# An attention and gated-MLP kernel: the first batch's weight preparation, the sums of its tiles, LayerNorm's small operations and the last batch's order

## The chip, the cores and the metric

The kernel runs on one core of one Trainium2 chip. Its five engines work in parallel, each through its own instructions in order: TensorE (PE in the profile; its weight loads are PEld), VectorE (DVE), ScalarE (ACT), GpSimd (POOL) and SyncE (SP), whose queue issues all DMAs here. The metric is the device time of one execution in microseconds (us); the median of three runs is given.

## What is computed

Eight batches of block-causal attention (8 heads, 576 positions, 64 per head), then a gated MLP with a spatial mixing matrix. Cut to what matters:

```python
scores = q @ k.T / 8                      # per batch and head, masked by blocks of 64
attn = exp(scores - max) ; attn = attn / (sum(attn) + 1e-9)
x = attn @ v                              # heads side by side: 576 x 512
h = maximum(x @ w_in, 0)                  # 512 -> 1024
u, v = h[:, :512], h[:, 512:]
v_n = (v - mean(v)) / sqrt(var(v) + 1e-6)
v_s = w_spatial @ v_n + b_spatial[:, None]
out = (u * v_s) @ w_out                   # 512 -> 512
```

w_in and w_out arrive as 64-bit floats. The kernel splits every operand of the MLP's matrix products into a high and a low part and adds three products (high x high, high x low, low x high).

## The kernel before

**Pairs and tiles.** Heads go in pairs: 8 batches x 4 pairs, numbered 0 to 31 here. A pair has nine score tiles (TILES, line 45): one for both heads' last 64 queries, and four of 128 queries for each head.

**Batch 0's attention** is a loop over 36 tiles (lines 821 to 845). Each step n issues one tile (`scores`, line 286: matmul, then on VectorE the masked maximum, on ScalarE the exponent with its row sum, on VectorE an addition and a reciprocal, on GpSimd the division), a few steps of "background" work, and the transposes of the tile five steps back (three from step 30 on). `av_lo` and `av_hi` make x of the pair. The two smallest tiles of a head share one sum; each other tile has its own. The order of these instructions on an engine is left to a scheduler that works by priority and estimated times.

**Background.** `spread` gives a generator a first and a last step. v's columns of w_in are prepared in steps 5 to 28, u's in 34 to 37, w_spatial in 40 to 47, w_out in 46 to 52; the last two fall behind the loop. Each block of 128 rows is loaded into one of two staging buffers (`stage`, tags gh and gl, which later hold the gates), decoded by four VectorE instructions (lines 152 to 165), cast on ScalarE (129) and subtracted on GpSimd (131).

**Batches 1 to 7's attention.** For a pair, `scores_8` (two matmuls, L518) is issued during the groups of the pair before, `scores_run` (L540) issues the other eight tiles in a row; `top` (L487, L494) takes maximum and exponent, `norm` (L502, L505, L508) the sums and the division. `turn_blocks` transposes on VectorE (L579 to L588), `regroup` moves the result by four DMAs on SP (L595, pb to ptt), and `av_pair` (L607) of that pair follows the scores of the next one. Scores and av take PSUM banks from a ring of six (`bank`, line 469), so av's first matmul waits until VectorE has read the bank's former scores.

**The MLP of a batch** runs in groups of matmuls between the scores of the next batch: five v groups (`v_group`; the fifth, v4, for the last 64 positions, L651), eight u groups (`u_group`, L711), eight spatial groups (`sp_group`, L735 to L740) and eight output groups (`out_group`, L761), the last two in halves z. A v group goes on in later calls: statistics (L662, L663 on VectorE), then logarithm and exponent on ScalarE (L665, L666) and four operations of one column on VectorE (L667 to L679), then the normalisation (L684), a cast (L690) and the low part on GpSimd (L691). The groups share two PSUM banks. A spatial group's result is multiplied with u (L742), cast (L745) and subtracted (L746) into gh and gl, which the output groups read.

`issue` (line 851) calls one group and takes the groups behind it one step further; `in_order` chains the instructions of each engine by hand in the order in which they were written, without the background's. `moe` returns the groups by pair. For batch 0 those are [v0, v1, v2, u0, v4], [v3, u1 to u5], [u6, u7, four spatial], [four output, four spatial], and four output groups for the next batch's first pair. Pair 4's scores stand ahead of the first v group.

Of the kernel before, what the change touches and what calls it, by code (L numbers as in the profile page):

```python
# [51 lines left out]
def kernel(  # L52
# [66 lines left out]
    staged = []

    def stage(name):

        tag = ("gh", "gl")[len(staged) % 2]
        staged.append(name)
        t = ff_p.tile([P, ND, HT], F32R, tag=tag, name=f"r{name}")
        return t.bitcast(F32).rearrange("p c t -> p (c t)")

    def split(hi, lo, raw):
# [2 lines left out]
        nc.gpsimd.tensor_tensor(out=lo, in0=raw, in1=hi.bitcast(F32), op=ALU.subtract)  # L131
        yield

    def prep_w(hi, lo, w, rows, cols, name):

        n = cols.stop - cols.start
        r = stage(name)
        if w.dtype == F32:
            nc.sync.dma_start(r[:, :n], w[rows, cols])
            yield  # L140
            yield from split(hi, lo, r[:, :n])
            return
        ri = r[:, :2 * n].bitcast(I32)
        nc.sync.dma_start(ri, w[rows, cols].bitcast(I32))
        words = ri.rearrange("p (n two) -> p n two", two=2)
# [6 lines left out]
        nc.vector.tensor_scalar(
            out=f, in0=high.bitcast(F32), scalar1=2.0**-112, scalar2=1.0,
            op0=ALU.mult, op1=ALU.mult,
        )
        yield
        nc.vector.tensor_scalar(
            out=low, in0=low, scalar1=29, scalar2=None, op0=ALU.logical_shift_right
        )
        yield  # L160
        nc.vector.scalar_tensor_tensor(
            out=fi, in0=fi, scalar=3, in1=low, op0=ALU.logical_shift_left, op1=ALU.bitwise_or
        )
        yield
        nc.vector.scalar_tensor_tensor(
            out=fi, in0=high, scalar=-(2**31), in1=fi, op0=ALU.bitwise_and, op1=ALU.bitwise_or
        )
# [3 lines left out]
    def prep_w_in(c, z):
        cols = slice(z * DH, (z + 1) * DH)
        yield from prep_w(
            wi_hi[:, c, cols], wi_lo[:, c, cols], w_in, slice(c * P, (c + 1) * P), cols,
            f"wi_{c}_{z}",
        )

    def prep_w_out(c):
        yield from prep_w(
            wo_hi[:, c, :], wo_lo[:, c, :], w_out, slice(c * P, (c + 1) * P), slice(0, DO),  # L180
            f"wo_{c}",
        )

    def prep_w_sp(c):
        r = stage(f"ws_{c}")[:, :S]
        nc.sync.dma_start(r, w_spT[c * P:(c + 1) * P, :])
# [99 lines left out]
    def scores(b, pr, i):  # L286
        hd, t = TILES[i]
        nm = f"{b}_{pr}_{i}"
        nmax = st_p.tile([P, 2], F32, tag="nmax", name=f"nmax_{nm}")
        if t != 1:  # L290
            sums[0] = st_p.tile([P, 4], F32, tag="ssum", name=f"ssum_{nm}")
        ssum = sums[0]
        sc = 1 if t == 1 else 0
# [35 lines left out]
        nc.vector.reciprocal(ssum[:, 2:3 + sc], ssum[:, 0:sc + 1])
        for k in range(sc, -1, -1):  # L330
            pk = ptiles[(b, pr, i - k)]
            nk = n if k == 0 else n - P
# [285 lines left out]
    def moe(b):  # L618
# [10 lines left out]
        def v_group(c):  # L629
# [16 lines left out]
            else:  # L646
# [17 lines left out]
            yield  # L664
            nc.scalar.activation(st[:m, 8:9], st[:m, 7:8], AF.Ln, bias=eps[:m, :])  # L665
            nc.scalar.activation(st[:m, 9:10], st[:m, 8:9], AF.Exp, scale=-0.5)  # L666
            nc.vector.tensor_scalar(  # L667
                out=st[:m, 10:11], in0=st[:m, 7:8], scalar1=EPS_LN, scalar2=-0.5,
                op0=ALU.add, op1=ALU.mult,
            )  # L670
            nc.vector.tensor_scalar(
                out=st[:m, 11:12], in0=st[:m, 9:10], scalar1=st[:m, 9:10], scalar2=st[:m, 10:11],
                op0=ALU.mult, op1=ALU.mult,
            )
# [45 lines left out]

        def sp_group(z, dc):
            if dc == 0:
                g[z] = (
                    ff_p.tile([P, ND, HT], F32R, tag="gh", name=f"gh_{b}_{z}"),
                    ff_p.tile([P, ND, HT], F32R, tag="gl", name=f"gl_{b}_{z}"),
                )
# [4 lines left out]
            n = 0
            for k in range(FULL):
                vh, vl = vn[k]
                for (a, w) in ((vh, ws_hi), (vh, ws_lo), (vl, ws_hi)):
                    mm(  # L735
                        ps[:, :HT], a[:, ds], w[:, k, zs], start=(n == 0), stop=False
                    )
# [7 lines left out]
            nc.scalar.copy(gh[:, dc, :], uz)  # L745
# [231 lines left out]
```

## Time and profile before

| | us |
|---|---|
| median of 3 runs | 717.19 (717.02 to 717.21) |
| the profiled execution | 718.89 |
| its span, first to last instruction | 717.1 |
| TensorE busy | 676.9 |
| VectorE busy | 468.9 |
| ScalarE busy | 383.5 |
| GpSimd busy | 275.7 |
| mean granted TensorE clock | 0.990 |

Rows of the profile read: line, engine, operation, output <- input, and for groups the count, the busy time in us and the mean of one in ns. In a timeline the two leading numbers are start and duration in us; brackets give the idle time of the engine just before and what ended it. In a row of a stretch each engine has its busy time and its number of instructions; then come the granted clock, the DMA engines' busy share and GB/s.

### The profile page before, as it was taken

How to read it: one execution, taken by the hardware profiler on the slowest of the kernel's cores; microseconds unless marked ns; L12 is line 12 of the kernel's file. 1: busy time of each engine (PE TensorE's matmuls, PEld its weight loads, DVE VectorE, ACT ScalarE, POOL GpSimd, SP SyncE). 2: the span in 40 equal slices, each digit the busy share in tenths (PEclk: the TensorE clock that was granted, in tenths of full speed). 3: DMA queues.
4: the chain of work that ended last, by engine and by line, in shares of the span. 5: the costliest groups of instructions: out<-in, count | busy, mean ns of one | idle time of the engine just before them, and what ended most of it. 6: DMA issues, size and time to landing. Idle time of an engine off the chain costs nothing. (4 is left out here: it accounts for less than half of the span.)

```text
span 717.1 us, 14166 instructions
## 1 busy us (share of the span) xinstructions
PE 676.9 (94%) x4864; PEld 573.4 (80%) x4864; DVE 468.9 (65%) x1755; ACT 383.5 (53%) x1088; POOL 275.7 (38%) x428
## 2 busy tenths in 40 slices
PE   8999687899999999999999999999999999999997
PEld 5555576787888878898788878898788877998997
DVE  5995578746766678556866767566876567661511
ACT  5878465443754457434664447445674447542621
POOL 4768345421444333332343414432354314430221
PEclk9999989999999999999999999999999999999999
DMA  6444634666455556666455666556456664543001
GB/s 226 141 143 140 168 70 142 154 170 156 107 132 131 151 151 146 145 127 172 105 128 141 172 163 144 129 123 157 107 137 160 164 177 101 128 84 105 1 26 41
DMA packets 37531, 94.40 MB, mean 132 GB/s; under 512 B 4178, under 2 KB 12882, under 8 KB 37460
## 3 DMA queue, kind: packets, MB, share of 16 engines
q1 hardware_dynamic: 37460, 93.51, 51.3%
q8 instruction: 38, 0.62, 0.3%
q14 instruction: 33, 0.27, 0.1%
HBM read 38.18 MB, written 9.44 MB: 66 GB/s over the span
## 5 line engine op out<-in xcount | busy, mean ns | idle before, releaser
L508 POOL TENSOR_SCALAR p<-p,sst 128x384 f32<-128x384 f32 (+4 forms) x252 | 136.5, 555 | 170.1 <-DVE sst L505 89.3
L494 ACT ACTIVATE p<-p,sst 128x384 f32<-128x384 f32 (+4 forms) x252 | 144.6, 575 | 77.1 <-DVE sst L487 71.7
L487 DVE CUSTOM_DVE_ANT_0 p<-s,mask 128x384 f32<-128x384 f32 (+4 forms) x252 | 108.2, 478 | 28.3 <-PE s L518 24.3
L607 PE MATMUL av<-ptt,v 128*64 128x32 f32 (+4 forms) x1120 | 89.2, 313 | 26.8 <-DVE sst L487 23.2
L711 PE MATMUL mu<-x,wi_hi 128*128 128x288 f32 x512 | 109.3, 297 | 0.9 <-ACT u L716 0.9
L607 PEld LDWEIGHTS av<-ptt,v 128*64 128x64 f32 x1120 | 69.1, 140 | 48.2 <-DVE sst L487 26.6
L742 DVE TENSOR_TENSOR u<-ms,u 128x288 f32<-128x288 f32 x64 | 29.1, 457 | 108.3 <-PE ms L740 108.3
L586 DVE STREAM_TRANSPOSE pb<-p 128x384 f32<-128x384 f32 (+1 forms) x224 | 89.8, 443 | 0.0
L746 POOL TENSOR_TENSOR gl<-u,gh 128x288 fp32r<-128x288 f32 x48 | 38.5, 803 | 132.5 <-ACT gh L745 132.5
L640 PE MATMUL mv<-wi_hi,x 128*128 128x512 f32 x256 | 86.4, 400 | 0.0
L711 PEld LDWEIGHTS mu<-x,wi_hi 128*128 128x128 f32 x512 | 84.1, 188 | 2.7 <-ACT u L716 1.1
L735 PE MATMUL ms<-ws_hi,vh 128*128 128x288 f32 x256 | 79.0, 309 | 1.7 <-ACT u L716 1.6
L691 POOL TENSOR_TENSOR vl<-vr,vh 128x512 fp32r<-128x512 f32 x32 | 41.1, 1284 | 92.4 <-ACT vh L690 92.4
L735 PE MATMUL ms<-ws_hi,vl 128*128 128x288 f32 x256 | 75.4, 294 | 0.0
L735 PE MATMUL ms<-ws_lo,vh 128*128 128x288 f32 x256 | 75.3, 294 | 0.0
L540 PE MATMUL s<-raw 64*128 64x512 f32 (+1 forms) x448 | 71.3, 444 | 0.9 <-DVE x L407 0.9
L711 PE MATMUL mu<-x,wi_lo 128*128 128x288 f32 x256 | 69.7, 295 | 0.0
L745 ACT CAST gh<-u 128x288 fp32r<-128x288 f32 x64 | 25.9, 428 | 79.5 <-DVE u L742 79.5
L540 PEld LDWEIGHTS s<-raw 64*128 64x128 f32 x448 | 42.2, 186 | 28.3 <-issue 17.8
L767 ACT COPY o<-mo 128x288 f32<-128x288 f32 x64 | 25.6, 400 | 65.0 <-PE mo L761 59.6
L761 PE MATMUL mo<-gh,wo_hi 128*128 128x288 f32 x256 | 57.1, 303 | 3.2 <-ACT gh L745 3.2
L640 PEld LDWEIGHTS mv<-wi_hi,x 128*128 128x128 f32 x256 | 48.1, 188 | 10.1
(127 smaller groups left out, 1383.2 us busy)
## 6 DMA issues: line engine op xcount, KB each, us to landing
ptt<-pb SPq DMA_DIRECT2D x112, 400.0 KB, 6.9
raw<-qk SPq DMA_DIRECT2D x31, 608.0 KB, 5.5
v<-v SPq DMA_DIRECT2D x32, 320.0 KB, 5.0
outT<-o SPq DMA_DIRECT2D x64, 144.0 KB, 2.0
rwi<-w_in SPq DMA_DIRECT2D x8, 512.0 KB, 4.0
rwo<-w_out SPq DMA_DIRECT2D x4, 512.0 KB, 4.6
rws<-w_spT SPq DMA_DIRECT2D x4, 288.0 KB, 2.8
rwt<-w_spT SPq DMA_DIRECT2D x2, 144.0 KB, 2.7
```

The source lines that it names most:

```text
L487: nc.vector.tensor_tensor_reduce(out=p[:, at:at + n], in0=ps, in1=mk, scale=-0.125, scalar=BIG if m == 0 else st[:, k:k + 1], op0=ALU.add, ...
L494: nc.scalar.activation(p, p, AF.Exp, bias=mx, scale=-1.0, accum_out=st[:, 10 + k:11 + k])
L508: nc.gpsimd.tensor_scalar(out=p, in0=p, scalar1=st[:, k:k + 1], scalar2=1.0, op0=ALU.mult, op1=ALU.mult)
L540: mm(ps[(t, hd)], raw[js, S + t * P:S + (t + 1) * P], raw[js, :n], start=True, stop=True,)
L586: nc.vector.transpose(to(hd * XH + 32 * t, [[P, m], *dims] if m > 1 else dims), p[:, :m * P])
L607: mm(to[js, :, PA - C_N[c]:], vt[:, c, js], ptt[:, 2 * z:2 * z + 2, at:at + C_N[c]], start=(c == 0), stop=(c == 4),)
L640: mm(ps, xs[k][:, j, cs], w[:, k, DH:], start=(n == 0), stop=(n == 3 * NC - 1),)
L691: nc.gpsimd.tensor_tensor(out=vl, in0=vr, in1=vh.bitcast(F32), op=ALU.subtract)
L711: mm(ps[:, :HT], w[:, k, ds], xs[k][:, j, zs], start=(n == 0), stop=(n == 3 * NC - 1),)
L735: mm(ps[:, :HT], a[:, ds], w[:, k, zs], start=(n == 0), stop=False)
L746: (nc.vector if dc == ND - 1 else nc.gpsimd).tensor_tensor(out=gl[:, dc, :], in0=uz, in1=gh[:, dc, :].bitcast(F32), op=ALU.subtract)
L761: mm(ps[:, :HT], w[:, k, es], a[:, k, :], start=(n == 0), stop=(n == 3 * ND - 1),)
```

## The change

- **Sums.** In batch 0's attention the addition and the reciprocal are made for groups of tiles: tile 0, tiles 1 to 4, 5 and 6, 7 and 8 (SUMMED). The divisions of a group follow its last tile.
- **Weights.** In the loop: v's columns and w_spatial's last rows in steps 5 to 29, w_spatial's loads in 9 to 14 into the buffer of u, its splits in 18 to 34, the loads of u's columns in 36 to 39 (two blocks into gh and gl, two into u's buffer). u's block c is decoded whole behind group c of the MLP (0 to 3). w_out comes in eight halves of a block: the load of half j behind group j + 7, its decode behind group j + 9, staged in the three buffers vr; the decode's temporary has two buffers of its own.
- **Order of batch 0's groups.** v0, v1 and v2 stand ahead of pair 4's scores, with `scores_8` of pair 4 between them. Then come [v3, v4, u0 to u3], [u4 to u7, four spatial], [four output, two spatial], [two spatial, three output], and one output group. All of this is chained by `in_order`.
- **LayerNorm.** L667 to L679 run on GpSimd in all batches; in batch 0 the normalisation follows in the same call.
- **Last batch.** All eight spatial groups stand ahead of the output groups, and the second half's gates have a buffer of their own (tag pb).

```diff
+    SUMMED = {0: (0,), 4: (1, 2, 3, 4), 6: (5, 6), 8: (7, 8)}
...
-        if t != 1:
-            sums[0] = st_p.tile([P, 4], F32, tag="ssum", name=f"ssum_{nm}")
+        of = next(x for x in SUMMED.values() if i in x)
+        if i == of[0]:
+            sums[0] = st_p.tile([P, 8], F32, tag="ssum", name=f"ssum_{nm}")
...
-        if t == 0:
+        if i != of[-1]:
             return
...
-        f = ff_p.tile([P, 512], F32, tag="vr", name=f"f{name}", bufs=3)[:, :n]
+        f = ff_p.tile([P, 512], F32, tag="f", name=f"f{name}", bufs=2)[:, :n]
...
+    def prep_u(c):
+        hi, lo, w = block(wi_hi, wi_lo, w_in, c, U_COLS)
+        for _ in parts(hi, lo, staged.pop(("u", c)), w, f"wu_{c}"):
+            pass
...
+    def fetch_out(j):
+        r = staged["o", j] = ff_p.tile([P, DH], F32, tag="vr", name=f"rwo_{j}", bufs=3)
+        fetch(r, out_block(j)[2])
...
-            nc.vector.tensor_scalar(
+            nc.gpsimd.tensor_scalar(
                 out=st[:m, 10:11], in0=st[:m, 7:8], scalar1=EPS_LN, scalar2=-0.5,
...
-            yield
+            if b:
+                yield
             nc.scalar.activation(
                 vr[:m, :], vr[:m, :], AF.Identity, bias=st[:m, 13:14], scale=st[:m, 12:13]
...
+                if b == B - 1 and z:
+                    t = pt_p.tile([P, 8 * XH], F32R, tag="pb", name="g_last")
+                    t = t[:, :2 * ND * HT].rearrange("p (x d t) -> p x d t", x=2, d=ND)
+                    g[z] = (t[:, 0], t[:, 1])
...
         if b == 0:
-            first = [[*vs[0:3], us[0], vs[4]], [vs[3], *us[1:6]], us[6:] + sp[0]]
-        else:
-            first = [
-                [vs[0], vs[4], us[0]], [vs[1], us[1], vs[2], us[2], vs[3], us[3]], us[4:] + sp[0]
+            return [
+                vs[:3], [vs[3], vs[4], *us[:4]], us[4:] + sp[0], out[0] + sp[1][:2],
+                sp[1][2:] + out[1][:3], out[1][3:],
             ]
-        return [*first, out[0] + sp[1], out[1]]
+        if b == B - 1:
+            return [[vs[0], vs[4], us[0], vs[1], us[1], vs[2], us[2], vs[3], us[3]], us[4:],
+                    sp[0] + sp[1], out[0], out[1]]
...
-    spread(chain([prep_w_in(c, 1) for c in range(NC)]), 7 * NC + 1, 5, 28)
-    spread(chain([prep_w_in(c, 0) for c in range(NC)]), 7 * NC + 1, 34, 37)
-    spread(chain([prep_w_sp(c) for c in range(FULL)] + [prep_w_tail()]), 3 * FULL + 5, 40, 47)
-    spread(chain([prep_w_out(c) for c in range(ND)]), 7 * ND + 1, 46, 52)
+    spread(chain([prep_v(c) for c in range(NC)] + [prep_w_tail()]), 7 * NC + 6, 5, 29)
+    spread(fetch_sp(), FULL + 1, 9, 14)
+    spread(prep_sp(), 2 * FULL + 1, 18, 34)
+    spread(fetch_u(), NC + 1, 36, 39)
...
+    for c in range(NC):
+        plan(c, prep_u, c)
+    for j in range(2 * ND):
+        plan(j + 7, fetch_out, j)
+        plan(j + 9, prep_out, j)
...
-    run(ahead)
-    mlp = moe(0)
+    for f in mlp.pop(0):
+        issue(f)
+        next(ahead, None)
```

More of the change, by code (lines that the diff above doesn't have):

```diff
@@ L117, with stage, fetch @@
     nc.gpsimd.memset(ws_b[64:97, :].bitcast(F32), 0.0)
[L119 to L124, printed above, removed]
+    def stage(tag, name):
         t = ff_p.tile([P, ND, HT], F32R, tag=tag, name=f"r{name}")
         return t.bitcast(F32).rearrange("p c t -> p (c t)")
+    def fetch(r, w):
+        n = w.shape[1]
+        if w.dtype == F32:
+            nc.sync.dma_start(r[:, :n], w)
+        else:
+            nc.sync.dma_start(r[:, :2 * n].bitcast(I32), w.bitcast(I32))
     def split(hi, lo, raw):
@@ L132, in split, with parts @@
         yield
-    def prep_w(hi, lo, w, rows, cols, name):
-        n = cols.stop - cols.start
-        r = stage(name)
+    def parts(hi, lo, r, w, name):
+        n = w.shape[1]
         if w.dtype == F32:
-            nc.sync.dma_start(r[:, :n], w[rows, cols])
-            yield
             yield from split(hi, lo, r[:, :n])
             return
-        ri = r[:, :2 * n].bitcast(I32)
-        nc.sync.dma_start(ri, w[rows, cols].bitcast(I32))
-        words = ri.rearrange("p (n two) -> p n two", two=2)
+        words = r[:, :2 * n].bitcast(I32).rearrange("p (n two) -> p n two", two=2)
         low, high = words[:, :, 0], words[:, :, 1]
-        f = ff_p.tile([P, 512], F32, tag="vr", name=f"f{name}", bufs=3)[:, :n]
+        f = ff_p.tile([P, 512], F32, tag="f", name=f"f{name}", bufs=2)[:, :n]
         fi = f.bitcast(I32)
-        yield
         nc.vector.tensor_scalar(
@@ L169, in prep_w, with block @@
         yield from split(hi, lo, f)
[L171 to L186, printed above, removed]
-        yield
-        yield from split(ws_hi[:, c, :], ws_lo[:, c, :], r)
+    def block(hi, lo, w, c, cols):
+        return hi[:, c, cols], lo[:, c, cols], w[c * P:(c + 1) * P, cols]
@@ new lines, with prep_v, fetch_sp @@
+    V_COLS, U_COLS = slice(DH, DFF), slice(0, DH)
+    G_TAGS = ("gh", "gl")
+    def prep_v(c):
+        hi, lo, w = block(wi_hi, wi_lo, w_in, c, V_COLS)
+        r = stage(G_TAGS[c % 2], f"wv_{c}")
+        fetch(r, w)
+        yield
+        yield from parts(hi, lo, r, w, f"wv_{c}")
+    spatial = []
+    def fetch_sp():
+        r = ff_p.tile([P, ND, S], F32, tag="u", name="rws")
+        for c in range(FULL):
+            nc.sync.dma_start(r[:, c, :], w_spT[c * P:(c + 1) * P, :])
+            yield
+        spatial.append(r)
@@ new lines, in prep_sp, with fetch_u @@
+    def prep_sp():
+        for c in range(FULL):
+            yield from split(ws_hi[:, c, :], ws_lo[:, c, :], spatial[0][:, c, :])
+    staged = {}
+    def fetch_u():
+        both = None
+        for c in range(NC):
+            if c < 2:
+                r = stage(G_TAGS[c], f"wu_{c}")
+            else:
+                if both is None:
+                    both = ff_p.tile([P, ND, S], F32, tag="u", name="wu_23")
+                    both = both.rearrange("p c t -> p (c t)")
+                r = both[:, (c - 2) * ND * HT:(c - 1) * ND * HT]
+            fetch(r, w_in[c * P:(c + 1) * P, U_COLS])
+            staged["u", c] = r
+            yield
@@ new lines, in prep_u, with out_block, prep_out @@
+    def prep_u(c):
+        hi, lo, w = block(wi_hi, wi_lo, w_in, c, U_COLS)
+        for _ in parts(hi, lo, staged.pop(("u", c)), w, f"wu_{c}"):
+            pass
+    def out_block(j):
+        return block(wo_hi, wo_lo, w_out, j // 2, slice(j % 2 * DO // 2, (j % 2 + 1) * DO // 2))
+    def fetch_out(j):
+        r = staged["o", j] = ff_p.tile([P, DH], F32, tag="vr", name=f"rwo_{j}", bufs=3)
+        fetch(r, out_block(j)[2])
+    def prep_out(j):
+        hi, lo, w = out_block(j)
+        for _ in parts(hi, lo, staged.pop(("o", j)), w, f"wo_{j}"):
+            pass
@@ L190, in prep_w_tail @@
     def prep_w_tail():
-        r = stage("wt")
+        r = stage(G_TAGS[0], "wt")
         for j in range(2):
@@ L322, in scores @@
         )
-        ptiles[(b, pr, i)] = pt
-        if t == 0:
+        ptiles[(b, pr, i)] = pt[:, :n]
+        if i != of[-1]:
             return
+        m = len(of)
         nc.vector.tensor_scalar(
-            out=ssum[:, 0:sc + 1], in0=ssum[:, 0:sc + 1], scalar1=EPS_SM, scalar2=None, op0=ALU.add
+            out=ssum[:, 0:m], in0=ssum[:, 0:m], scalar1=EPS_SM, scalar2=None, op0=ALU.add
         )
[L329 to L332, printed above, removed]
+        nc.vector.reciprocal(ssum[:, 4:4 + m], ssum[:, 0:m])
+        for k, j in enumerate(of):
+            pk = ptiles[(b, pr, j)]
             nc.gpsimd.tensor_scalar(
-                out=pk[:, :nk], in0=pk[:, :nk], scalar1=ssum[:, 2 + sc - k:3 + sc - k],
-                scalar2=1.0, op0=ALU.mult, op1=ALU.mult,
+                out=pk, in0=pk, scalar1=ssum[:, 4 + k:5 + k], scalar2=1.0,
+                op0=ALU.mult, op1=ALU.mult,
             )
@@ L722, in sp_group @@
             if dc == 0:
[L723 to L726, printed above, removed]
+                if b == B - 1 and z:
+                    t = pt_p.tile([P, 8 * XH], F32R, tag="pb", name="g_last")
+                    t = t[:, :2 * ND * HT].rearrange("p (x d t) -> p x d t", x=2, d=ND)
+                    g[z] = (t[:, 0], t[:, 1])
+                else:
+                    g[z] = tuple(
+                        ff_p.tile([P, ND, HT], F32R, tag=x, name=f"{x}_{b}_{z}") for x in G_TAGS
+                    )
             gh, gl = g[z]
@@ L776, in moe @@
         if b == 0:
[L777 to L782 removed]
+            return [
+                vs[:3], [vs[3], vs[4], *us[:4]], us[4:] + sp[0], out[0] + sp[1][:2],
+                sp[1][2:] + out[1][:3], out[1][3:],
+            ]
+        if b == B - 1:
+            return [[vs[0], vs[4], us[0], vs[1], us[1], vs[2], us[2], vs[3], us[3]], us[4:],
+                    sp[0] + sp[1], out[0], out[1]]
+        return [
+            [vs[0], vs[4], us[0]], [vs[1], us[1], vs[2], us[2], vs[3], us[3]], us[4:] + sp[0],
+            out[0] + sp[1], out[1],
+        ]
     pairs = [(b, pr) for b in range(B) for pr in range(NPAIR)]
@@ L849, with plan @@
     behind = []
+    issued = 0
+    then = {}
+    def plan(at, f, *args):
+        then.setdefault(at, []).append(lambda: f(*args))
+    for c in range(NC):
+        plan(c, prep_u, c)
+    for j in range(2 * ND):
+        plan(j + 7, fetch_out, j)
+        plan(j + 9, prep_out, j)
     def issue(f):
-        nonlocal n
+        nonlocal issued
         gen = f()
@@ L859, in issue @@
         behind.append(gen)
+        for x in then.pop(issued, []):
+            x()
+        issued += 1
         in_order()
-        step_background(n)
-        pass_over()
-        n += 1
     pass_over()
+    mlp = moe(0)
     ahead = scores_8(*pairs[NPAIR])
-    run(ahead)
-    mlp = moe(0)
+    for f in mlp.pop(0):
+        issue(f)
+        next(ahead, None)
     rest = []
```

11 lines of the change are left out of this document (5 added, 6 removed).

## The prediction

> **What bounds the kernel now.** I read the page first, then the span by batch (busy time in stretches), then TensorE's waits by stretch, then the timeline at each long wait. The page's first part, and TensorE's row of its slices (tenths of 17.9 us each):
>
> ```profile
> PE 676.9 (94%) x4864; PEld 573.4 (80%) x4864; DVE 468.9 (65%) x1755; ACT 383.5 (53%) x1088; POOL 275.7 (38%) x428
> PE   8999687899999999999999999999999999999997
> ```
>
> TensorE is busy for 676.9 of 717.1 us; no other engine is near. The change removes no matmul, so its worth is found in 40.2 us of idle TensorE, and in matmuls that ran at a reduced clock. The dip is in slices five and six, the first MLP batch; the other batches look alike. One of them (stretches view: span, then PE, PEld, DVE, ACT, POOL), then TensorE's waits around the dip (us in total, times, longest), and after it:
>
> ```profile
> 215.00:300.00 85.00, 82.45 (x620) 71.45 (x620) 58.06 (x221) 45.42 (x131) 31.84 (x52) 1.00 0.59 144
> PE av L607 <- DVE sst L487: 10.5, 3, 6.9
> PE mu L711 <- ACT u L716: 0.9, 1, 0.9
> ...
> PE av L607 <- DMA ptt<-pb: 3.0, 3, 2.3
> ```
>
> So an ordinary batch loses 2.55 us, and the first 10.5 + 0.9 + 3.0 = 14.4. The 6.9 us wait and what led to it (timeline: start, us, operation, idle before it and its releaser; then two stretches, with the granted clock behind POOL's count):
>
> ```profile
> 79.99 0.43 DVE L157 TENSOR_SCALAR rwo<-rwo 128x512 int32<-128x512 int32 x1 [3.42 <-DMA rwo<-w_out]
> 86.01 0.27 DVE L671 TENSOR_SCALAR st<-st 128x1 f32<-128x1 f32 x1 [3.01 <-ACT st L666]
> 90.83 5.76 PE L607 MATMUL av<-ptt,v 128*64 128x288 f32 x40 [6.92 <-DVE sst L487]
> ...
> 87.00:89.00 2.00, 0.00 (x0) 0.00 (x0) 1.90 (x7) 1.97 (x4) 0.74 (x1) 0.50 0.88 310
> ...
> 113.00:115.00 2.00, 0.00 (x0) 0.00 (x0) 1.64 (x6) 0.40 (x2) 0.38 (x1) 1.00 1.00 367
> ```
>
> VectorE, which works in order, sat 3.42 us at w_out's decode for its load and 3.01 us at L671 for ScalarE's exponent (L666). Scores behind these held their PSUM banks, and av_pair wants a bank. The clock fell to 0.50, and the 40 av matmuls took 5.76 us. Ordinary batches have the same kind of wait, smaller:
>
> ```profile
> 339.31 0.13 DVE L667 TENSOR_SCALAR st<-st 128x1 f32<-128x1 f32 x1
> 339.76 0.27 DVE L671 TENSOR_SCALAR st<-st 128x1 f32<-128x1 f32 x1 [0.31 <-ACT st L666]
> 340.45 0.68 DVE L662 BATCH_NORM_STATS2 st<-vr 64x6 f32<-64x512 f32 x1
> 341.26 0.65 DVE L487 CUSTOM_DVE_ANT_0 p<-s,mask 128x512 f32<-128x512 f32 x1
> 341.97 1.88 PE L607 MATMUL av<-ptt,v 128*64 128x288 f32 x22 [1.48 <-DVE sst L487]
> ...
> 359.67 0.27 DVE L671 TENSOR_SCALAR st<-st 128x1 f32<-128x1 f32 x1 [1.77 <-ACT st L666]
> 362.14 2.06 PE L607 MATMUL av<-ptt,v 128*64 128x288 f32 x22 [0.65 <-DVE sst L487]
> ```
>
> **The change part by part.**
>
> **1. LayerNorm's four small operations (L667 to L679) go from VectorE to GpSimd.** At 339.31 they delay the next statistics to 340.45, 1.14 us, and through the first score tile (341.26) the bank. Without them av starts 1.14 earlier: 0.34 of the 1.48 stays. At 359.67 VectorE idled 1.77 us for the same reason, so all 0.65 could go; but av would then meet its own transfer (part 4), so I count 0.5. Batches 1 to 6 each have both: 6 x 1.64 = 9.8 us (bounds 3 and 10.7). GpSimd's price isn't shown; its nearest rows (groups by shape, 300 to 640 us):
>
> ```profile
> L508 POOL TENSOR_SCALAR p<-p,sst 128x512 f32<-128x512 f32 x34 | 23.1, 691 | 37.6 <-DVE sst L505 33.9 <-ACT p L494 3.8
> ...
> L508 POOL TENSOR_SCALAR p<-p,sst 128x128 f32<-128x128 f32 x34 | 12.6, 371 | 0.0
> ```
>
> The line through 691 and 371 ns gives 0.26 us for one column; three behind the exponent make 0.8 us, about VectorE's own 0.69 (339.76 to 340.45). I take no loss (bounds: 0.26 to 0.37 each); GpSimd's 38% and, in batches above 0, one group of matmuls between these and their reader (L684) are the cover. Without it, see the third rival.
>
> **2. The last batch's spatial groups stand together, with own gate buffers.** The two waits:
>
> ```profile
> 692.31 0.40 PE L761 MATMUL mo<-gh,wo_hi 128*128 128x288 f32 x1 [1.08 <-ACT gh L745]
> ...
> 707.52 0.40 PE L761 MATMUL mo<-gh,wo_hi 128*128 128x288 f32 x1 [1.08 <-ACT gh L745]
> ```
>
> Each output group started on gates just made. With four spatial groups, then four output groups in between, both go: -2.2 us. What follows the last matmul stays. The new buffer's (pb) last reader was done long before.
>
> **3. The attention of batch 0, and v0's start.** Fewer sums and, up to v0, no decode of u relieve VectorE (three sums fewer in each pair), but TensorE's instructions stand without a gap from 20 to 50 us (its slices show 9), so little comes of it there: 0 (bounds -2 to +4: a grouped sum is normalised up to three tiles later, and lag 3 in pair 3 leaves little room). At the end (groups from 53.7 to 68.2, timeline rows around them):
>
> ```profile
> 51.86 1.77 PE L301 MATMUL s<-raw 64*128 64x384 f32 x4
> ...
> L540 PE MATMUL s<-raw 64*128 64x512 f32 (+3 forms) x16 | 4.7, 460 | 0.9 <-DVE x L407 0.9
> L518 PE MATMUL s<-raw 128*128 128x288 f32 x4 | 1.1, 406 | 0.0
> ...
> 68.20 0.50 PE L640 MATMUL mv<-wi_hi,x 128*128 128x512 f32 x1
> ```
>
> Pair 4's scores (4.7 + 1.1) move behind v groups, so v0 starts 5.8 us earlier, near 62.4. They are paid later at some 2.4 + 0.8, the lower price of scores issued in a row. Net -2.6 (0 to -4).
>
> **4. Batch 0's MLP.** The 14.4 us of waits go, and the clock's 2.8 us (half of 5.76): -17.2. What is late next? Rows for TensorE's groups, for one decode (four instructions, 68 to 130 us), and one of them in the crowded attention stage:
>
> ```profile
> 76.49 1.13 PE L518 MATMUL s<-raw 128*128 128x288 f32 x4
> 79.04 0.40 PE L651 MATMUL mv<-wi_hi,xs 128*128 128x512 f32 x1
> 81.00 2.90 PE L540 MATMUL s<-raw 64*128 64x512 f32 x16
> 698.59 0.30 PE L735 MATMUL ms<-ws_hi,vh 128*128 128x288 f32 x1
> 700.46 0.29 PE L735 MATMUL ms<-ws_hi,vh 128*128 128x288 f32 x1
> ...
> L165 DVE SCALAR_TENSOR_TENSOR fwo<-rwo,fwo 128x512 int32<-128x512 int32 x4 | 3.0, 746 | 0.0
> L161 DVE SCALAR_TENSOR_TENSOR fwo<-fwo,rwo 128x512 int32<-128x512 int32 x4 | 2.7, 683 | 0.0
> L157 DVE TENSOR_SCALAR rwo<-rwo 128x512 int32<-128x512 int32 x4 | 1.9, 469 | 3.4 <-DMA rwo<-w_out 3.4
> L152 DVE TENSOR_SCALAR fwo<-rwo 128x512 f32<-128x512 f32 x4 | 1.7, 424 | 5.4 <-POOL vl L691 2.5 <-DMA rwo<-w_out 1.8 <-POOL wo_lo L131 1.1
> ...
> L161 DVE SCALAR_TENSOR_TENSOR fwi<-fwi,rwi 128x512 int32<-128x512 int32 x8 | 6.7, 838 | 0.0
> ```
>
> Three v groups take 8.3 us (68.20 to 76.49), v4 2.0, a run of scores 2.4 to 2.9, a spatial group of 14 matmuls 1.87, so a u or output group of 12 1.6. From v0's start, T, TensorE does v0, score 8, v1, v2 (9.0), pair 4's scores (11.7), v3, v4 (16.4) and at T + 17.2 needs the last quarter of u's weights. VectorE in order: score 8's maximum (T + 4.6), v0's statistics and a decode of 2.2 (7.6), sums, v1's statistics and a decode (10.9), pair 4's maxima and first turns, some 6.2 (17.1), v2's statistics and the last decode (20.1); the cast and the subtraction follow, 22.0. A **new wait of 4.6 us** at u0 (bounds 0 and 9), and its clock: the wait around 113 to 115 us left the clock at 1.00, the one of 6.9 halved it; I take 1.3 us, half of 2.8.
> The Trainium skill, "GPSIMD Engine Reference", section Specifications, says that GpSimd's SBUF interfaces are shared with VectorE, contended by two-input and two-port VectorE instructions; 838 ns against 683 agrees. By that price the wait is some 2 us longer.
> The Trainium skill, "TensorE: Matmul & The Clock Gate", section Why this matters for your kernels, warns of idle gaps over about 3 us; the 6.92 gap agrees. By it the full 2.8 us of clock would be lost behind my 4.6.
>
> w_out's halves are loaded two groups ahead, on SP, ahead of the regroup DMAs; their decode (8 x 1.1 us) lies on VectorE beside u4 to u7 and the spatial groups, 13.9 us of TensorE. With the 14.5 us of a mean pair (58.06 / 4) VectorE is full there and 1 to 3 us late at the end. The pairs behind have fewer groups: 6, 5, and 4 with batch 1's first, so with 6.4 us for scores and av 16.5, 15 and 14 us of TensorE. For a pair's transfer (the run of scores, its regroup on SP; the issues of one regroup, and their landing):
>
> ```profile
> 154.47 2.43 PE L540 MATMUL s<-raw 64*128 64x512 f32 x16
> 165.71 5.92 SPq L595 DMA_DIRECT2D ptt<-pb x4
> ...
> L595 SPq DMA_DIRECT2D ptt<-pb x4: 555/1282/2803, 352.7 to 356.8; - x4
> DMA to landing us min/median/max: 5.8/6.7/7.2
> ```
>
> Regroup starts 11.2 us after the scores, its last issue is 4.1 later, landing 6.7 more: 22 us, while av's second half comes 4 us into the next pair. A pair shorter than 18 us waits. 1.5, 3 and 4 would be due; each wait lengthens the pair for the next, and VectorE starts up to 1.4 us sooner than in the row, so I take 5.0 in all (0 to 8.5).
>
> Batch 0's MLP: -17.2 + 4.6 + 1.3 + 5.0 = -6.3.
>
> **Sum.** -9.8 - 2.2 - 2.6 - 6.3 = -20.9. It is made on the profiled span of 717.1 (that execution took 718.9); the median of the runs shown is 717.2, and I carry the difference over: 717.2 - 20.9 = 696.3, so **696 us**.
>
> **Rivals.**
> - *The gap only moves.* Decodes on GpSimd's crowded port, a full clock loss, full transfer waits: 4.6 + 2.7, 2.8, 8 in place of 10.9, so 717.2 - 20.9 + 7.2, some 703.5. For it: VectorE's list ends 5 us after TensorE's. Against: all loads are ahead. 0.14.
> - *Behind the freed bank another wait stands* (transfers, av's halves): part 1 gives 2 instead of 9.8, 704. For it: 352.7 + 4.1 + 6.7 is 363.5, av's second half in that pair starts near 363.7. Against: the 1.48 wait has a landed transfer. 0.08.
> - *Slower: GpSimd's chain holds ScalarE.* L684 waits for GpSimd, in order behind a vl or a normalisation of 0.7 us and more; behind L684 stand copies that free TensorE's two MLP banks. 40 v groups; from 0.52 us each (20.9/40) the change loses. At 0.75 each: 726. Against: the group between, GpSimd's idle share. 0.05. The Trainium skill, "GPSIMD Engine Reference", section Engine selection, gives elementwise work to VectorE; no run here shows such an operation of one column on GpSimd.
> - *It doesn't do what it says:* u's decode costs batch 0 all it gains and the bank waits stay: 715 to 717. 0.03.
>
> **How the numbers follow.** The forecast has 0.70. Its own bounds, unknown costs not all at one end, reach from 688 to 703; the range to 708 takes in the first two rivals. Left out are the last two and tails, near 0.2. Faster by over 0.2% (1.4 us, about what can be told here): 0.70 + 0.14 + 0.08 = 0.92; within it 0.03; slower 0.05.
>
> **What would show it.** L671 on GpSimd and no VectorE wait on L666; av's waits in batches 1 to 6 near 0.4; no wait at the two last output starts; v0 near 62; one TensorE wait of 3 to 6 us at u0 for a weight's lo or hi part; three waits of 1 to 2 us on ptt after it. Wrong, if v0 starts after 66, if u0 waits over 8 us, or if av's waits on scores stay at 2.1 a batch.

## The result, and the profile after

The changed kernel takes 754.85 us (median of 4 runs, 753.61 to 756.11), the kernel before beside it 717.2. The ratio is 1.052, interval 1.049 to 1.055: 37 us slower, where 21 us less was forecast. The profiled execution took 756.11 us, its span 754.3. Its page (busy time; then TensorE's and the clock's slices, of 18.9 us each):

```profile
PE 695.7 (92%) x4864; PEld 584.4 (77%) x4864; DVE 443.9 (59%) x1587; ACT 382.2 (51%) x1092; POOL 318.4 (42%) x592
PE   8899579698898999899998999899998999899998
...
PEclk9789879799999999999999999999999999999999
```

The dip of the first MLP batch is wider, not gone, and the same 4864 matmuls are busy 18.8 us longer, for the most part by a lower clock. Where it lies, by three stretches of the same work: up to av of pair 8, up to av of pair 31, the rest. First the changed kernel, then the one before (length, then busy time of PE, PEld, DVE, ACT, POOL, and the clock):

```profile
0.00:198.90 198.90, 167.45 (x976) 121.32 (x977) 128.66 (x447) 105.05 (x297) 95.85 (x156) 0.90 0.47 132
198.90:687.70 488.80, 467.57 (x3465) 406.57 (x3465) 303.53 (x1117) 254.17 (x742) 207.02 (x405) 0.99 0.55 136
687.70:754.30 66.60, 60.72 (x425) 56.53 (x424) 11.73 (x26) 22.96 (x54) 15.49 (x31) 0.99 0.08 27
```

```profile
0.00:177.40 177.40, 157.34 (x978) 115.53 (x978) 127.77 (x475) 102.91 (x290) 88.31 (x128) 0.96 0.54 150
177.40:651.40 474.00, 459.13 (x3464) 401.40 (x3464) 325.20 (x1235) 257.44 (x744) 177.07 (x289) 1.00 0.57 139
651.40:717.10 65.70, 60.42 (x425) 56.50 (x424) 15.93 (x46) 23.20 (x54) 10.30 (x11) 1.00 0.08 27
```

Batch 0 got 21.5 us longer (11.4 of them idle, 10.1 longer busy), the six ordinary batches 14.8 (6.4 idle, 8.4 longer busy), the tail 0.9. If the clock's cost is taken as half of TensorE's busy time under a clock of 0.5, it is 15.7 us in batch 0 against 4.6 before, and 6.8 in the ordinary batches against none. VectorE has 21.7 us less to do in the ordinary batches and 4.2 less in the tail (0.9 more in batch 0), and that bought no time.

**Ordinary batches.** The wait at av in which 1.48 us were lost is 0.33 now, as forecast. A new one stands a pair later (timeline of the changed kernel: the end of u5's matmuls, then the rows of v3's chain):

```profile
309.26 0.69 PE L755 MATMUL mu<-x,wi_hi 128*128 128x288 f32 x4
...
310.26 0.29 ACT L708 ACTIVATE st<-st,eps 128x1 f32<-128x1 f32 x1
...
310.58 0.20 ACT L709 ACTIVATE st<-st 128x1 f32<-128x1 f32 x1
...
310.78 1.63 POOL L551 TENSOR_SCALAR p<-p,sst 128x256 f32<-128x256 f32 x4 [0.78 <-ACT st L709]
...
312.38 0.30 POOL L463 TENSOR_SCALAR xs<-x 128x128 fp32r<-128x128 f32 x1
312.74 0.19 POOL L710 TENSOR_SCALAR st<-st 128x1 f32<-128x1 f32 x1
313.04 0.34 POOL L714 TENSOR_SCALAR st<-st 128x1 f32<-128x1 f32 x1
313.49 0.27 POOL L718 TENSOR_SCALAR st<-st 128x1 f32<-128x1 f32 x1
313.85 0.26 POOL L722 TENSOR_SCALAR st<-st 128x1 f32<-128x1 f32 x1
...
314.15 0.81 ACT L728 ACTIVATE vr<-vr,st 128x512 f32<-128x512 f32 x1 [3.06 <-POOL st L722]
...
315.52 0.70 ACT L760 ACTIVATE u<-mu 128x288 f32<-128x288 f32 x2
...
315.97 0.40 PE L784 MATMUL ms<-ws_hi,vh 128*128 128x288 f32 x1 [2.08 <-ACT u L760]
```

The exponent was ready at 310.78. GpSimd works in order: four divisions and the copy of x's tail first, then the four operations, 1.4 us with the gaps. ScalarE holds at L728 for 3.06 us, and behind it stand the two evacuations of u that TensorE needs for a bank. ScalarE's waits for this chain (in total, times, longest), after, then before:

```profile
ACT vr L728 <- POOL st L722: 62.6, 33, 4.6
```

```profile
ACT vr L684 <- DVE st L679: 17.9, 26, 1.3
```

**Batch 0.** TensorE's three long waits, all in u0 (ahead of its first, seventh and eighth matmul), and what held them, from the engines' timelines (VectorE's last decode of u, ScalarE, GpSimd, TensorE):

```profile
90.82 0.40 DVE L150 TENSOR_SCALAR fwu<-wu 128x512 f32<-128x512 f32 x1
...
92.33 0.69 DVE L163 SCALAR_TENSOR_TENSOR fwu<-wu,fwu 128x512 int32<-128x512 int32 x1
```

```profile
87.60 0.57 ACT L688 ACTIVATE vr<-mv 128x512 f32<-128x512 f32 x1
...
93.19 0.81 ACT L728 ACTIVATE vr<-vr,st 128x512 f32<-128x512 f32 x1 [4.60 <-POOL st L722]
...
94.56 0.61 ACT L133 CAST wi_hi<-fwu 128x512 fp32r<-128x512 f32 x1
```

```profile
88.22 0.61 PE L755 MATMUL mu<-x,wi_hi 128*128 128x288 f32 x1 [3.54 <-ACT vr L688]
95.22 0.61 PE L755 MATMUL mu<-x,wi_hi 128*128 128x288 f32 x1 [5.19 <-ACT wi_hi L133]
97.27 0.61 PE L755 MATMUL mu<-x,wi_lo 128*128 128x288 f32 x1 [1.44 <-POOL wi_lo L135]
```

10.2 us in all: 3.54 for a bank and 6.6 for the last quarter of u's weights. v3's relu (87.60) frees the bank late, behind pair 4's eight exponents; u's last decode begins at 90.82 behind pair 4's turns. Later w_out: SP's queue, VectorE and TensorE.

```profile
122.93 5.91 SPq L638 DMA_DIRECT2D ptt<-pb  x4
128.93 7.58 SPq L130 DMA_DIRECT2D rwo<-w_out  x4
```

```profile
134.74 0.29 DVE L150 TENSOR_SCALAR fwo<-rwo 128x256 f32<-128x256 f32 x1 [6.73 <-DMA rwo<-w_out]
```

```profile
136.57 0.61 PE L784 MATMUL ms<-ws_hi,vh 128*128 128x288 f32 x1 [4.80 <-DVE u L791]
```

The fifth half's load is issued behind pair 5's regroup, VectorE sits 6.73 us at its decode, and the gate products behind it hold TensorE's banks.

### The profile page after: what moved, and what is told of

It reads as the page before. It is cut to its first block, busy times and chain, and to the rows that moved or that the text cites. A ratio compares the mean times of both kernels' runs of the same rounds, so it can differ in the third digit from the quotient of the medians.

```text
span 754.3 us, 14080 instructions
## 1 busy us (share of the span) xinstructions
PE 695.7 (92%) x4864; PEld 584.4 (77%) x4864; DVE 443.9 (59%) x1587; ACT 382.2 (51%) x1092; POOL 318.4 (42%) x592
## 5 line engine op out<-in xcount | busy, mean ns | idle before, releaser
L755 PE MATMUL mu<-x,wi_hi 128*128 128x288 f32 x512 | 114.0, 304 | 13.3 <-ACT wi_hi L133 5.2
L784 PE MATMUL ms<-ws_hi,vh 128*128 128x288 f32 x256 | 82.4, 322 | 19.5 <-ACT u L760 14.7
L755 PEld LDWEIGHTS mu<-x,wi_hi 128*128 128x128 f32 x512 | 86.5, 192 | 17.9 <-ACT u L760 6.5
L795 POOL TENSOR_TENSOR gl<-u,gh 128x288 fp32r<-128x288 f32 x45 | 36.5, 810 | 113.2 <-ACT gh L794 113.2
L784 PE MATMUL ms<-ws_hi,vl 128*128 128x288 f32 x256 | 78.3, 306 | 0.0
L784 PE MATMUL ms<-ws_lo,vh 128*128 128x288 f32 x256 | 78.3, 306 | 0.0
L755 PE MATMUL mu<-x,wi_lo 128*128 128x288 f32 x256 | 71.3, 300 | 1.4 <-POOL wi_lo L135 1.4
L784 PEld LDWEIGHTS ms<-ws_hi,vh 128*128 128x128 f32 x256 | 51.0, 199 | 22.3 <-ACT u L760 16.5
L583 PEld LDWEIGHTS s<-raw 64*128 64x128 f32 x448 | 41.6, 189 | 29.4 <-issue 18.9
L728 ACT ACTIVATE vr<-vr,st 128x512 f32<-128x512 f32 (+1 forms) x40 | 32.5, 813 | 62.6 <-POOL st L722 62.6
L794 ACT CAST gh<-u 128x288 fp32r<-128x288 f32 x60 | 24.3, 428 | 71.9 <-DVE u L791 71.1
```

The lines of the kernel that those rows point to most:

```text
L583: mm(ps[(t, hd)], raw[js, S + t * P:S + (t + 1) * P], raw[js, :n], start=True, stop=True,)
L728: nc.scalar.activation(vr[:m, :], vr[:m, :], AF.Identity, bias=st[:m, 13:14], scale=st[:m, 12:13])
L755: mm(ps[:, :HT], w[:, k, ds], xs[k][:, j, zs], start=(n == 0), stop=(n == 3 * NC - 1),)
L784: mm(ps[:, :HT], a[:, ds], w[:, k, zs], start=(n == 0), stop=False)
L795: (nc.vector if dc == ND - 1 else nc.gpsimd).tensor_tensor(out=gl[:, dc, :], in0=uz, in1=gh[:, dc, :].bitcast(F32), op=ALU.subtract)
```

## The experiments

Each kernel was timed beside the kernel before; ratios are compared (0.01 is 7.2 us), since the medians of before lie between 716.99 and 718.36. Waits are TensorE's, from each run's trace.

**a_dve**: the changed kernel with `nc.vector` at L710 to L722.

> The changed kernel with LayerNorm's four small operations back on VectorE in all batches; nothing else is undone. Theory A (GpSimd's chain holds ScalarE, and ScalarE holds TensorE's MLP banks): the 14.7 us that batches 1 to 6 gained go, the 2.6 us of new waits in the last batch go, and of batch 0's 21.6 us some 8, those that hang on the two waits of L728 for GpSimd (2.60 and 4.60 us): 754.8 - 25 = 730, and the waits of u4 to u7 and of the first spatial group on ScalarE in each batch are gone. Theory B (u's decode behind the v groups is the cost, the four operations are harmless): at most 5 us less, 750. Theory C (the prediction's part 1 holds, another part hides it): slower by some 10 us, 765.

733.86 us, 1.0242 (1.0221 to 1.0262): 20 us less by the ratios. Theory A holds for the ordinary batches (the waits of 2.1 us are gone, av's 1.48 is back) and C falls. In the two profiled executions, 22.4 us apart, the ordinary batches hold 12.9 of the difference, the tail 3.6 and batch 0 5.9. Of those 5.9 us, 4.1 lie ahead of the end of v0's matmuls (66.94 against 71.05), where none of the four operations runs: behind two waits in attention (1.10 and 1.41 us here, 1.60 and 1.41 in the changed kernel) the clock stood at 0.5 for 3.41 us here and for 13.65 there. So the 20 us are not all the operations' (see the next run).

**a_dve0**: VectorE in batch 0 alone.

```diff
-            nc.gpsimd.tensor_scalar(
+            (nc.gpsimd if b else nc.vector).tensor_scalar(
```

> The changed kernel with the four small operations on VectorE in batch 0 only. Theory A: some 8 us less, 747, with batches 1 to 7 as in the changed kernel (period 82.9 to 85.3). Theory B: within 3 us of 754.8, since ScalarE and VectorE would still reach u's last decode as late.

755.69 us, 1.0547 (1.0507 to 1.0588): nothing. So batch 0's loss isn't GpSimd's, though the trace names it there: waits of 4.31 and 5.24 us stand in u0 all the same, for v3's relu and u's cast. The 4.60 us at L728 were a wait that had another right behind it. In batch 0 this kernel and a_dve are alike, and yet it took 198.2 us there and a_dve 193.0: here too the clock in attention stood at 0.5 for 13.65 us. Some 5 of a_dve's 20 us are therefore this stretch of clock, which none of the runs explains.

**b_gps**: the kernel before with `nc.gpsimd` at L667 to L679.

> The kernel before with only the four small operations moved to GpSimd. Theory A: batches 1 to 6 lose some 14.7 us, the last batch 2.6, batch 0 (which keeps the group between exponent and reader here) 0 to 5: 734 to 740. Theory C, the prediction's part 1: 717.2 - 9.8 = 707.4. Theory B: 705 to 717.

731.12 us, 1.0191 (1.0166 to 1.0217). Each ordinary batch loses av's waits (1.48 to 0.33, 0.65 to almost nothing) and gets 0.46 and 2.12 us instead; three of these are followed by a reduced clock. By the same stretches, the ordinary batches are 12.1 us longer here and the tail 3.7, near the 12.9 and 3.6 of a_dve, and batch 0 is 2.9 shorter. So the two kernels agree on theory A outside batch 0.

**b_last**: the kernel before with the last batch's order.

```diff
+        if b == B - 1:
+            return [[vs[0], vs[4], us[0], vs[1], us[1], vs[2], us[2], vs[3], us[3]], us[4:],
+                    sp[0] + sp[1], out[0], out[1]]
```

> The kernel before with only the last batch's order and its own gate buffers. The prediction's part 2: both waits of 1.08 us go, 717.2 - 2.2 = 715.0. Rival: the order brings waits of its own on ScalarE in the last batch (as the four new ones of 0.89, 0.16, 0.67 and 0.84 us in the changed kernel), 717 to 717.6.

714.97 us, 0.9968 (0.9951 to 0.9985). Part 2 holds. The four waits of the changed kernel's tail aren't the order's: TensorE's only listed wait from 640 us on is this one, ahead of the last av.

```profile
645.62 0.40 PE L766 MATMUL mo<-gh,wo_hi 128*128 128x288 f32 x1 [1.08 <-ACT gh L750]
```

**m1** and **m1c**: b_last with GpSimd for some groups.

```diff
-            nc.vector.tensor_scalar(
+            (nc.gpsimd if c < 3 and b < B - 1 else nc.vector).tensor_scalar(
```

m1c has `c >= 3` in its place.

> The kernel before with the last batch's order and own gate buffers, and with the four small operations on GpSimd only for v0, v1 and v2 and only in batches 0 to 6; v3, v4 and the last batch stay on VectorE. Theory A, narrowed: only v3's four stand behind a whole run of scores' normalisations on GpSimd and make the waits of 2.1 and 0.46 us per batch; v0's and v2's bring the gain of 2.1 us per batch at av. So 715.0 - 6 x 2.1 = 702.4, with batch 0 as it is. Rival: every group on GpSimd holds ScalarE and VectorE's free time is worth nothing: 715 or more.

> The complement: the kernel before with the last batch's order, and with the four operations on GpSimd only for v3 and v4 in batches 0 to 6. Theory A, narrowed: av's waits of 1.48 and 0.65 us stay as they are, the waits of 2.1 and 0.46 us at the spatial groups come in 6 batches, 15.5 us, and a clock window of 3.41 us at 0.5 behind some of them, 1.7 us each: 730 to 737. Rival: the waits come from v0 to v2: 715.

m1: **706.7 us, 0.9852 (0.9837 to 0.9867), faster than both kernels**. m1c: 724.35 us, 1.0096 (1.0070 to 1.0123). So v3 and v4 carry the loss and v0 to v2 the gain; both are smaller than expected. First two of m1c's waits in an ordinary batch, then m1's in all:

```profile
280.26 3.02 PE L607 MATMUL av<-ptt,v 128*64 128x288 f32 x40 [1.46 <-DVE sst L487]
291.21 0.40 PE L740 MATMUL ms<-ws_hi,vh 128*128 128x288 f32 x1 [1.32 <-ACT u L716]
```

```profile
PE av L607 <- DVE sst L487: 10.9, 10, 4.2
PE av L607 <- DMA ptt<-pb: 4.2, 4, 1.4
...
PE ms L740 <- ACT u L716: 1.3, 4, 0.4
```

In m1c the wait at the spatial group is 1.3 us in place of 2.1, no reduced clock follows one, and the second av's wait grows from 0.65 to 1.5. In m1 the first av of an ordinary batch waits 0.33 us (1.48 before), but the second still waits 0.8 to 1.4, in four batches of six for its own transfer now. Between the av of pairs 8 and 31 m1 needs 4.0 us less than b_last, and batch 0 gives another 3.6 in the profiled executions; as batch 0 differs by 2.5 us there between b_last and the kernel before, which are alike in it, the 3.6 are less certain. In the ordinary batches the two parts, -4.0 and +10.6, come to less than b_gps's +12.1; its three stretches of reduced clock, which neither has, cost 5.1.

**c_u**: a_dve with u's decode in the attention stage (its generator as before, steps 34 to 37).

> The changed kernel with the four operations on VectorE, and u's weights fetched and decoded in the attention stage as before (steps 34 to 37) in place of behind v0 to v3. Theory B (u's last decode stands on VectorE behind pair 4's maxima, turns and v2's small operations, and on ScalarE behind eight exponentials): the waits at u0 (4.49, 5.71 and 0.74 us) go, and with them 3.6 us of reduced clock in the window of 13.65 us; the attention stage gets some 2.3 us longer: 733.9 - 14.5 + 2.3 = 721.7. Rival: VectorE is simply full there, and whatever leaves the groups comes back as the same wait in attention or at w_out: 730 to 734.

732.85 us, 1.0222 (1.0199 to 1.0245): within the uncertainty of a_dve's 1.0242. Theory B falls as it was put. The wait at u0 shrank to 1.13 us, but u1 waited 4.86 for the bank of v4, whose evacuation stands on VectorE behind the same turns, and the attention stage got longer (v0's last matmul ended at 72.2, not 66.9). Part of that is not the decode: behind the same waits of 1.10 and 1.41 us the clock stood at 0.5 for 13.65 us in c_u's profiled execution and for 3.41 in a_dve's. So this pair of runs can't price the decode; c_sum and c_sumu below, without such a stretch, can.

**c_uwo**: c_u with w_out's loads earlier.

```diff
+        if j < 4:
+            if j % 2 == 0:
+                pair_of[0] = stage(G_TAGS[j // 2], f"wo_{j}")
+            r = pair_of[0][:, j % 2 * DH:(j % 2 + 1) * DH]
...
+        ((0, 7), (0, 8), (1, 9), (1, 10), (7, 11), (8, 12), (9, 13), (12, 15))
```

> As the run before, and w_out's first four halves loaded into the two free gate tiles at the first two v groups, the next three before pair 5's regroup on SP, the last behind it. Theory: the wait of 5.11 us at a spatial group is w_out's fifth half, whose load stands on SP behind the regroup (VectorE idle 7.04 us for it); it goes with some 1.7 us of clock, and of the waits of 1.71 and 0.97 us at u on ScalarE's cast of w_out about half: 721.7 - 8 = 713.5. Rival: VectorE is the bound in that pair, and the wait turns into one on VectorE or at the next av: within 3 us of the run before.

728.81 us (723.64 to 732.47), 1.0155 (1.0104 to 1.0206). The 4.92 us at the spatial group are gone (0.42 left); av of pair 4 waits 3.42 instead of 0.96. About half of what was expected came through (5 us by the ratios, uncertain by 4). The profiled execution is the fastest of the four, and unlike c_u's it has no reduced clock in attention.

**c_v4**: c_uwo with v4 ahead of pair 4.

```diff
-                vs[:3], [vs[3], vs[4], *us[:4]], us[4:] + sp[0], out[0] + sp[1][:2],
+                [vs[0], vs[1], vs[4], vs[2]], [vs[3], *us[:4]], us[4:] + sp[0], out[0] + sp[1][:2],
```

> The run c_uwo with v4 moved ahead of pair 4's scores (v0, v1, v4, v2, then pair 4, v3, u0 to u3). Theory: with u's decode gone from there, the 4.85 us wait at u1 is for the PSUM bank of v4, whose evacuation on VectorE stands behind pair 4's maxima and turns; v4 ahead of them frees it: 4.85 us and 1.7 us of clock less, 728.8 - 6.5 = 722. Rival: VectorE is full from the first v group to w_out's last half, and the wait moves to the av of pair 4 (3.42 there now): 726 to 730.

727.2 us, 1.0127 (1.0099 to 1.0155), not told apart from c_uwo. The rival is nearer: 4.85 us for v4's bank became 4.27 for v3's and 2.41 for u's.

**c_sum**: a_dve with the sums of before.

```diff
-    SUMMED = {0: (0,), 4: (1, 2, 3, 4), 6: (5, 6), 8: (7, 8)}
+    SUMMED = {0: (0,), 2: (1, 2), 4: (3, 4), 5: (5,), 6: (6,), 7: (7,), 8: (8,)}
```

> The changed kernel with the four operations on VectorE and the attention stage's sums in the groups of before (t = 0 and 1 together, all others alone). Theory: TensorE's waits of 1.10 and 1.41 us near 28 and 31 us, for a normalisation on GpSimd, come from the grouping, since a grouped tile is normalised up to three tiles later; they and the clock window behind them (3.41 us here, 13.65 in the changed kernel) go: 733.9 - 2.5 - 1.7 = 729.7, and more where the longer window had come. Rival: they come from the spatial weights' split on GpSimd beside it (1.3 to 1.4 us each), and stay: 732 to 736.

728.27 us, 1.0139 (1.0112 to 1.0166). The grouped sums cost 7 us by the ratios, and v0 ends at 61.3 in place of 66.9 us. In the changed kernel's timeline stand two waits, and from 29.93 on a clock of 0.5 for 13.65 us; with the sums as before neither stands there, though the split on GpSimd does, so the rival falls:

```profile
28.56 0.55 PE L419 MATMUL t<-ident,p 128*128 128x128 f32 x3 [1.60 <-POOL p L376]
...
31.14 1.12 PE L474 MATMUL avl<-ptlo,v 128*64 128x256 f32 x2 [1.41 <-DVE x L450]
```

**m2**: m1 with w_out's loads two ahead, decodes in written order.

```diff
+        for c in range(ND):
+            yield from gens[c]
+            if c + 2 < ND:
+                next(gens[c + 2])
+                yield
```

> The run m1 with w_out's loads issued two ahead of their decodes, and the decodes held in the order written, the first behind pair 5's turns. Theory: in batch 0 VectorE's wait of 2.68 us for w_out's load, ahead of pair 5's maxima, goes; av of pair 4 waits some 1.5 in place of 4.24 us, and the clock window of 6.83 us behind it goes, 2.5 us: 706.7 - 5.2 = 701.5. Rival: the three decodes that now stand ahead of pair 6's maxima bring the same wait to av of pair 5 (3.52 there now): 705 to 709.

715.74 us, 0.9955 (0.9936 to 0.9975): 7 us slower than m1 by the ratios. The third weight's load is late, VectorE waits 5.74 us for it ahead of pair 6's maxima, and av of pair 5 waits 11.15. The rival, larger than expected.

**c_sumu**, **c_p4**, **c_sumuwo**, **m4**: combinations on c_sum.

> The run c_sum (VectorE for the four operations, sums grouped as before) with u's weights decoded in the attention stage as before. Theory B: the waits at u0 and u1 (4.23, 5.24 and 0.74 us) shrink to the 1.13 and 4.86 us that c_u showed, and the clock window of 13.65 us to 6.83: some 7 us less, and the attention stage 2 to 3 us longer, so 728.3 - 4.5 = 723.8. Rival D (VectorE and ScalarE have a fixed list of work before u1, and the decode costs in one place what it saves in the other): 727 to 730.

725.52 us, 1.0111 (1.0085 to 1.0137): 2.0 us by the ratios, between the two expectations. The waits are 1.13 and 4.86 us as expected; v0 ends 2.8 us later.

> The run c_sum with pair 4's scores ahead of v0, as in the kernel before, in place of behind v2; u's decodes stay behind v0 to v3. Theory E: pair 4's maxima and turns (some 6 us of VectorE) and its eight exponentials (4.4 us of ScalarE, ahead of v3's relu and of u's last cast) are what makes u0 late; ahead of v0 they are over in time, the waits of 4.23 and 5.24 us shrink to some 4 in all and the clock window with them, and 3.4 us of scores move ahead, where they are hidden by nothing: 728.3 - 6 = 722. Rival D: the same list in another order, 727 to 731.

732.32 us, 1.0209 (1.0179 to 1.0239). Theory E falls: the waits, all in u0 here as in c_sum, are 4.12, 3.95 and 0.74 us, 8.8 in all against 10.2, and the scores ahead have to be paid. Pair 4's place behind the v groups is a gain of 5 us here by the ratios.

> c_sumu with w_out's loads early as in c_uwo: the wait of 4.81 us at a spatial group goes with its clock window, part of it returns at av of pair 4 (3.42 us in c_uwo): 4 to 5 us below c_sumu. Rival D: within 2 us of c_sumu.

721.92 us, 1.0056 (1.0040 to 1.0071), 4 us below c_sumu, as expected.

> c_sumuwo with the four operations of v0, v1 and v2 on GpSimd in batches 1 to 6. By what m1 gained over b_last (8.3 us): 8 us below c_sumuwo, some 711. To beat m1 (706.7) it would have to gain in batch 0 as well, which no theory here expects.

717.74 us, 1.0001 (0.9977 to 1.0025): 4 us below c_sumuwo, half of what was expected and the ordinary batches' share of m1's gain. It doesn't beat m1.

## Why the prediction was wrong

By its own terms, each measured as a difference of ratios along one chain of kernels (changed, a_dve, c_sum, b_last, before; each difference uncertain by some 2 us):

| term | forecast, us | measured, us | from |
|---|---|---|---|
| 1, four operations on GpSimd | -9.8 | +20 | a_dve against the changed kernel |
| 2, last batch | -2.2 | -2.3 | b_last |
| 3, sums in the attention stage | 0 | +7.4 | c_sum against a_dve |
| 3, v0's start, and 4, batch 0's MLP | -2.6 - 6.3 | +12.3 | c_sum against b_last |
| sum | -20.9 | +37.3 | |

Some 5 us of the first row are the clock's in batch 0 and not the operations' (a_dve and a_dve0 above); 12.9 us lie in the ordinary batches, which the forecast of -9.8 was for. The last row of terms holds all else that the change does to batch 0, the spatial weights' new place among it.

**Part 1: sign wrong.** The operations cost what was estimated: L710 to L722 take 191, 338, 265 and 260 ns in their groups. The gain was there too, 1.15 us at the first av. What failed is the cover, "in batches above 0, one group of matmuls between these and their reader (L684)". For v3 the four operations are issued with u4, behind a whole run of scores, whose divisions GpSimd has in its queue, and the group between is u5. TensorE had finished u5 at 309.95 (309.26 + 0.69), before v3's exponent was ready at 310.78, so the group covered nothing. This is the third rival, which had 0.05; its price of 0.75 us for each v group was the wrong form: m1 and m1c show that v0 to v2 gain and v3 and v4 pay. And no clock was counted: 6.8 of the 14.8 us in ordinary batches.

**Part 2 was right.** What the tail lost again (0.89, 0.16, 0.67 and 0.84 us) is part 1's, since b_last and a_dve have none of it.

**Part 3: bound too narrow, and a start that was none.** The argument that the attention stage has no gap to lose was for a gain; a loss was bounded by 4 us and came to 7.4, because a division that comes late holds a transpose and the clock falls behind it. And v0 did start near 62, at 61.62, but the rows of v0 stand like this:

```profile
61.62 0.48 PE L683 MATMUL mv<-wi_hi,x 128*128 128x512 f32 x1
62.48 0.48 PE L683 MATMUL mv<-wi_lo,x 128*128 128x512 f32 x1
...
68.85 0.49 PE L683 MATMUL mv<-wi_lo,x 128*128 128x512 f32 x1
...
69.96 1.09 PE L683 MATMUL mv<-wi_hi,x 128*128 128x512 f32 x4
```

Transposes and av of the last attention pair lie between them. v0's last matmul ends at 71.05; before, 71.21. The mark was met and told nothing.

**Part 4: two steps failed.** "A new wait of 4.6 us at u0": it was 10.2 in three pieces, above the bound of 9, and not GpSimd's doing (a_dve0). VectorE's list was too short: it ran some 17 us from v0's end to the end of the last decode, and in c_sum that takes 24.2 (61.30 to 85.52). From v0's end to the last wait in u0, VectorE (third pair of numbers) is busy 22.27 of 26.3 us there and TensorE 16.09:

```profile
61.30:87.60 26.30, 16.09 (x73) 11.85 (x71) 22.27 (x68) 14.60 (x37) 13.51 (x15) 0.84 0.00 1
```

ScalarE was listed with the last cast alone; its eight exponents ahead of v3's relu held a bank, and VectorE sat 2.63 us there for an exponent of ScalarE's (L709). The first rival's crowded port shows there as well: beside GpSimd's vl (1.76 and 1.73 us in place of 1.3) the last operation of two decodes took 1.66 and 1.63 us in place of 0.69. The second: "w_out's halves are loaded two groups ahead, on SP, ahead of the regroup DMAs". That is so for four of the eight; the fifth is issued behind pair 5's regroup, and the wait of 4.8 us is its. Earlier loads gave 4 us (c_sumuwo against c_sumu), u's decode elsewhere 2 (c_sumu). The clock's term was mis-sized too: -2.8 + 1.3 were forecast, and it cost batch 0 11 us more than before, 4.5 of them ahead of v0's end. The term for late transfers came out near its size: 3.6 us in three waits on ptt, for 5.0.

**Still open** are some 6 us between c_sumuwo (1.0056) and b_last (0.9968); in the profiled executions 3.8 of them lie in batch 0 and 2.1 in the ordinary batches. Taking away one wait in batch 0 brought the next, for another bank (c_u, c_v4). That VectorE's list is simply too long until w_out is done is likely, but not shown: the one pair of runs in which it differs (the changed kernel and a_dve0, with and without the four operations off it) is equal in time, and there ScalarE had to wait for GpSimd instead. The spatial weights' split inside the attention loop, and batch 0's normalisation in the same call, were not tried alone.

## What to carry to other kernels

Before an operation goes to an idle engine, write down what that engine has in its queue at the moment when the operand is ready, and who waits in order behind the reader: GpSimd was idle 6 parts in 10, and still 3 us late for one group in five. Move only the groups whose readers have time (m1: 1.5% faster), and count a first start only with the end of the same group. A queue position is checked for each transfer of a row, not for the first.

## What the runs showed of the hardware

Short waits cost more than their length, and not each time. The six waits of 2.08 to 2.44 us in ordinary batches of the changed kernel: behind four of them the clock was 0.5 for 3.41 us, behind two it stayed at 1. Stretches behind two equal waits, with 25 and 16 matmuls in 3.4 us:

```profile
233.00:236.40 3.40, 3.40 (x25) 3.40 (x26) 0.46 (x1) 0.67 (x2) 1.22 (x2) 1.00 0.93 170
...
316.65:320.05 3.40, 3.40 (x16) 3.40 (x16) 0.46 (x1) 0.35 (x1) 0.31 (x1) 0.50 0.97 213
```

Which of them it is follows from their place. In each trace the stretches at 0.5 begin on a grid with a step of 3.41 us; a cell is the time from one grid point to the next (here the stretches begin at 316.65, 401.98, 487.31 and 654.57, which are 25, 25 and 49 steps apart). The wait ahead of 315.97 lies in one cell of that grid, with 1.32 us of matmuls in the cell; the wait ahead of 232.99 is cut by the grid point at 231.32, and both cells have more. The other four agree (2.03, 2.06 and 2.44 us idle in one cell; 570.41's wait is cut at 569.23):

```profile
227.91:231.32 3.41, 2.99 (x23) 2.76 (x21) 3.06 (x10) 0.35 (x2) 2.83 (x9) 1.00 0.00 0
231.32:234.73 3.41, 1.74 (x13) 1.74 (x14) 0.00 (x0) 1.89 (x4) 1.28 (x1) 1.00 0.69 107
...
313.24:316.65 3.41, 1.32 (x10) 1.09 (x10) 0.72 (x3) 2.04 (x4) 1.62 (x4) 1.00 0.40 44
```

Over the traces of all 17 kernels (from 12 us on), a cell at clock 1 in which TensorE idled 2.0 us or more was followed by a cell at 0.5 in 56 cases of 56, one with less than 1.4 us in none of some 3250, and between the two in 6 of 68. How long the clock then stays low is not told by this: 3.41 us in a_dve and 13.65 in c_u, behind the same two waits.

Behind the waits of 1.48 us of the kernel before, six times, no such stretch stands, nor behind m1c's eighteen of 1.3 to 1.5. The Trainium skill, "TensorE: Matmul & The Clock Gate", section Why this matters for your kernels, warns of gaps over about 3 us; here 2.1 us were enough in four cases of six, and the measurement decides.
